# Strassen's scheme for the second product of the last four blocks, with a transposed output stored in short runs

## The chip, the cores and the metric

The kernel runs on one core of one Trainium2 chip. A core has a matrix engine (TensorE, PE), a vector engine (VectorE, DVE), a scalar engine with the transcendental functions (ScalarE, ACT), a general engine (GpSimd, POOL) and an engine that here only issues transfers (SyncE, SP). They run side by side and wait for each other through semaphores. Each engine carries out its own instructions strictly in order. Transfers between DRAM and the on-chip SBUF are issued from a queue of SP, ACT or POOL and carried by 16 DMA engines. PE writes its sums into PSUM, eight banks of 128 x 512 floats. The metric is the device time of one execution, in microseconds (us).

## The reference

Two parts follow each other. The first is a linear attention over 8 batches, 8 heads, 576 positions and 64 features; the second is an RMS norm with a gated feed-forward layer over all 8 x 576 = 4608 tokens of 512 features (d_model), with 1536 hidden features (d_ff).

```python
q_s = softmax(q, over the features)             # exp(q - max) / (sum + 1e-9)
k_s = softmax(k, over the positions)
kv  = einsum('bhsd,bhse->bhde', k_s, v)         # 64 x 64 for each batch and head
x   = einsum('bhsd,bhde->bhse', q_s, kv)        # rearranged to 4608 x 512
xn  = x / sqrt(mean(x * x) + 1e-6) * rms_g
g   = xn @ w_gate                               # 512 x 1536
h   = g * 1 / (1 + exp(-g)) * (xn @ w_val)
out = h @ w_out                                 # 1536 x 512
```

All matrices are wanted in fp32 accuracy. The kernel writes each fp32 operand as a sum of two fp32r numbers, "hi" (a cast) and "lo" (the remainder, a subtraction), and makes a product from three: hi x hi, hi x lo and lo x hi.

## The kernel before

**Blocks and pairs.** The 4608 tokens are worked off in nine blocks of 512. Blocks 0 to 2 go one by one. Blocks 3 to 8 go as three pairs (p = 0, 1, 2; `NPAIR = 3`), and what follows is about them. Names such as `pp` or `put` are steps, each a Python function that issues a few instructions.

**First product of a pair, by Strassen's scheme.** xn of both blocks and the weights are cut in two by two parts. `pp` makes, for each of six groups i of hidden features (two tiles of 128 of each half) and each m (gate or value), seven products of six matmuls instead of eight (L1093). The sums of weights that this needs were made once while blocks 1 and 2 ran, and lie in DRAM ("wd"); `w_in` loads them on POOL's queue. The sums of the activations are `t_add` (L1037), cast and remainder are `b_hi` and `b_lo` (L1049). The results in PSUM are combined on DVE (`c_u2`, `c_u3`, `c_21` and the like, L1114, L1130), `gate` takes the silu on ACT and `hm` multiplies gate by value (L1150). So the hidden tile c (of 12) of block t stands in SBUF with the hidden features on the partitions and 512 tokens along them, 128x512; for t = 0 in tiles "gs", for t = 1 in tiles "xh", "xl" and "w".

**Second product of a pair, plain.** For each block t and hidden tile c, `hp_hi` casts the tile to "hh", `hp_lo` (L1162) makes the remainder "hl", `o_in` loads the tile's 128 x 512 output weights, hi and lo, 512 KB, on POOL's queue, and `f2p` (L1180) makes 12 matmuls: four output tiles of 128 tokens by three terms. After 12 hidden tiles the four sums stand in PSUM with tokens on the partitions. `put` copies each to a tile "ot" (or "gs" at the end, L385, L1193) and stores it with one transfer of 2 KB rows (L1199; for the very last one, two halves on SP's and ACT's queues, L1194 and L1196).

**What sets the order.** All steps stand in one long list, `ORDER`, under a manual schedule: each step is issued where the list has it, on the engine that its letter names (A, D or P for ACT, DVE or POOL). Nothing reorders them later. Tiles of a name come from a pool with a number of buffers ("ot" has 2, "hh" and "hl" 2, "gs" 3); a step that takes a tile whose buffer is still read waits for the reader. The second product of a pair is laced into the first product of the next: in the list, `f2p` steps of pair p stand between the `pp` steps of pair p + 1, and what is left stands alone.

Of the kernel before, what the change touches and what calls it, by code (L numbers as in the profile page):

```python
# [34 lines left out]
k_eps.0.2 q_load0.1.1 k_rec.0.2 q_x0.0.0 kv_norm0.0.3:D kv_norm0.0.2:A k_max.1.0 q_mul0.0.2:P conv_mul.0.2 q_t0.0.3
q_x0.0.1 x_sq.0.0 conv_shift.0.2 x_hi.0.0:A q_t0.0.2 q_c0.0.3:A warm.2.7 conv_mul.1.0 k_tr.1.0 load_w.1.2 q_x0.0.3
q_max0.1.0 x_hi.0.1:A load_w.3.1 q_c0.0.2:D warm.2.4 conv_low.0.2.1 q_sub0.1.0:P load_w.2.1 k_top.1.0 x_sq.0.1 q_x0.0.2
conv_shift.1.0 w_lo.0.1:P q_exp.1.0 x_lo.0.1 n_sum0.0 x_sq.0.3 load_w.2.2 x_lo.0.0 k_diag.1.0:A w_lo.0.0:P n_sum0.1
x_sq.0.2 q_sum0.1.0 x_hi.0.3:A k_rows.1.0 v_load.1.0 n_sum0.2 q_eps0.1.0 conv_low.1.0.2 conv_add.0.2.1 q_max0.1.1
n_sum0.3 q_rec0.1.0 k_sub.1.0 x_hi.0.2:A q_sub0.1.1:P warm.2.12 x_lo.0.3 k_exp.1.0 warm.2.9 n_t.0 conv_mul.2.0  # L40
conv_add.1.0.2 f1.0.0.0.0 f1.0.0.0.1 f1.0.0.0.2 o_hi.0:A n_y0.0 f1.0.0.0.3 f1.0.1.0.0 q_exp.1.1 load_w.4.0 f1.0.0.1.0
x_lo.0.2 f1.0.1.0.1 f1.0.1.0.2 load_w.3.2 f1.0.1.0.3 n_y1.0 f1.0.0.1.1 load_w.3.0 conv_low.2.0.2 f1.0.0.1.2 o_lo.0:P
f1.0.0.1.3 f1.0.1.1.0 f1.0.1.1.1 w_hi.1.0.2:A f1.0.1.1.2 q_load0.1.2 f1.0.1.1.3 q_mul0.1.0:P conv_shift.2.0 f1.0.0.2.0
f1.0.0.2.1 conv_mul.2.1 f1.0.0.2.2 n_rows.0 f1.0.0.2.3 f1.0.1.2.0 w_lo.1.0:P conv_mul.1.2 f1.0.1.2.1 conv_shift.2.1
f1.0.1.2.2 conv_low.1.2.1 f1.0.1.2.3 g_mul.0 conv_mul.4.1 conv_add.2.0.2 q_sum0.1.1 f1.1.0 silu.0 load_w.5.1
conv_shift.4.1 k_load.1.1 conv_shift.1.2 conv_mul.4.0 q_eps0.1.1 h_mul.0 conv_add.1.2.1 w_hi.2.0.2:A load_w.6.0
# [276 lines left out]
def linear_attention_then_gated_ffn(ctx: ExitStack, tc, q, k, v, w_gate, w_val, w_out, rms_g, out):  # L323
# [918 lines left out]
```

## Time and profile before

| | before |
|---|---|
| runs, us | 959.84, 960.16, 964.75 |
| median, us | 960.16 |
| profiled execution, us | 959.09 |
| span in it (first to last instruction), us | 957.2 |
| granted TensorE clock, mean | 0.996 |
| PE busy, us (matmuls) | 936.5 (4697) |
| DVE / ACT / POOL busy, us | 664.1 / 438.3 / 531.7 |

The stretches of the program by their busy time, in us (the program's phases overlap by some microseconds at their ends):

| stretch | PE | DVE | ACT | POOL |
|---|---|---|---|---|
| 0 to 528, blocks 0 to 2 with the attention | 511.3 | 443.6 | 343.7 | 392.7 |
| 528 to 600 | 72.0 | 59.4 | 32.7 | 34.9 |
| 600 to 744 | 144.0 | 70.9 | 26.7 | 49.6 |
| 744 to 888 | 144.0 | 65.3 | 23.5 | 40.4 |
| 888 to 957 | 65.2 | 25.0 | 11.7 | 14.1 |

A profile counts an engine as busy while an instruction of it runs. The "chain" that the text speaks of follows the last instruction of the program back in time, at each step to what released it. "SPq", "ACTq" and "POOLq" are the engines as issuers of transfers. In rows of instructions, `ot<-ps_o 128x512` means that a tile named ot was written from one named ps_o; the bracket behind some rows is the idle time ahead and the work that ended it.

### The profile page before, as it was taken

The page shows a single profiled execution, that of the slowest core. Times are in us where ns is not written, and L with a number is a line of the kernel's source. Part 1 is how long each engine was busy: PE and PEld are TensorE (multiplying, and loading weights), DVE is VectorE, ACT ScalarE, POOL GpSimd, SP SyncE. Part 2 cuts the span into 40 slices and gives each one's busy share as a digit, 9 for nine tenths or more (in the row PEclk, how much of TensorE's full clock was granted, in tenths as well). Part 3 has the DMA queues.
Part 4 walks back from the last instruction along what each step waited for, and adds up shares of the span by engine and source line. Part 5 has one row for each costly group of instructions (what it writes and reads, how often), then busy time and mean ns, then how long its engine had stood idle before and what let it go on. Part 6 is the DMA issues. An engine that isn't in the chain of part 4 may idle for free.

```text
span 957.2 us, 14051 instructions
## 1 busy us (share of the span) xinstructions
PE 936.5 (98%) x4697; PEld 761.8 (80%) x4697; DVE 664.1 (69%) x1424; ACT 438.3 (46%) x703; POOL 531.7 (56%) x551
## 2 busy tenths in 40 slices
PE   7999998999999999999999999999999999999998
PEld 5688886878878887887888888888888888888886
DVE  7899788988879987878887788643436644344442
ACT  5998746766657775565434454101113212111111
POOL 5897856865878887776655436333234311322123
PEclk9999999999999999999999999999999999999999
DMA  9986516889875899887795783756755857546455
GB/s 263 291 255 200 128 36 212 281 283 302 279 247 136 245 262 237 200 255 210 186 259 164 228 247 105 245 160 219 230 198 185 255 168 239 184 151 237 143 155 174
DMA packets 164435, 202.31 MB, mean 211 GB/s; under 512 B 105060, under 2 KB 126860, under 8 KB 159756
## 3 DMA queue, kind: packets, MB, share of 16 engines
q0 software_dynamic: 23232, 113.26, 37.6%
q1 hardware_dynamic: 140988, 88.04, 33.1%
q8 instruction: 37, 0.61, 0.3%
q14 instruction: 34, 0.28, 0.1%
q10 hardware_dynamic: 144, 0.13, 0.0%
HBM read 160.49 MB, written 40.89 MB: 210 GB/s over the span
## 4 chain that ended last, share of the span: by engine, by line
PE 79%; DVE 7%; DMA 7%; SPq 3%; ACT 2%; issue 1%; POOL 0%; DVEq 0%; ACTq 0%; POOLq 0%
PE ps_gv L1093 16%; PE ps_o L1093 12%; PE ps_gv L952 12%; PE ps_o L1180 10%; PE ps_o L989 7%; PE ps_a L1093 6%; PE ps_gv L1180 5%; PE ps_a L1180 5%; SPq L626 3%; DMA kt<-in_k_dram 2%; DMA qt<-in_q_dram 2%; PE ps_a L558 2%; DMA vt<-in_v_dram 1%; PE ps_a L764 1%; DMA w<-in_moe_w_val_dram 1%
## 5 line engine op out<-in xcount | busy, mean ns | idle before, releaser
L952 PE MATMUL ps_gv<-xh,w 128*128 128x512 f32 x576 | 190.2, 398 | 1.2 <-ACT ps_a L434 0.5
L1093 PE MATMUL ps_gv<-x,ring 128*128 128x512 f32 x576 | 142.6, 392 | 0.0
L952 PEld LDWEIGHTS ps_gv<-xh,w 128*128 128x128 f32 x576 | 108.1, 188 | 26.4 <-issue 1.1
L1093 PEld LDWEIGHTS ps_gv<-x,ring 128*128 128x128 f32 x576 | 107.2, 188 | 22.2
L952 PE MATMUL ps_gv<-xl,w 128*128 128x512 f32 x288 | 111.7, 391 | 0.0
L1066 POOL DMA_DIRECT2D ring<-wd x54 | 30.4, 564 | 128.7 <-PE ps_gv L1093 56.8
L1114 DVE TENSOR_TENSOR tmp<-tmp,ps_gv 128x512 f32<-128x512 f32 x84 | 57.2, 682 | 52.1 <-PE ps_gv L1093 49.7
L1093 PE MATMUL ps_o<-x,ring 128*128 128x512 f32 x360 | 84.9, 389 | 0.0
L1093 PEld LDWEIGHTS ps_o<-x,ring 128*128 128x128 f32 x360 | 67.6, 188 | 14.0
L989 PE MATMUL ps_o<-o,hh 128*128 128x512 f32 x288 | 74.9, 403 | 0.0
L385 ACT CAST hh<-gs 128x512 fp32r<-128x512 f32 x56 | 34.5, 616 | 78.1 <-DVE gs L1130 29.4
L952 PEld LDWEIGHTS ps_gv<-xl,w 128*128 128x128 f32 x288 | 54.2, 188 | 10.6 <-issue 0.4
L989 PEld LDWEIGHTS ps_o<-o,hh 128*128 128x128 f32 x288 | 53.3, 190 | 11.2 <-issue 0.4
L1114 DVE TENSOR_TENSOR tmp<-tmp,ps_o 128x512 f32<-128x512 f32 x42 | 28.7, 686 | 42.2 <-PE ps_o L1093 40.0
L876 POOL TENSOR_TENSOR w<-w,w 128x512 fp32r<-128x512 f32 x32 | 43.9, 1375 | 3.9 <-ACT w L385 3.5
L511 DVE TENSOR_REDUCE cm<-kt 116x128 f32<-116x640 f32 x28 | 36.8, 1313 | 4.2 <-DMA kt<-in_k_dram 4.1
L989 PE MATMUL ps_o<-o,hl 128*128 128x512 f32 x144 | 39.4, 396 | 0.3 <-POOL hl L973 0.3
L1162 POOL TENSOR_TENSOR hl<-gs,hh 128x512 fp32r<-128x512 f32 x22 | 28.5, 1298 | 17.0 <-DVE hh L385 9.8
L1180 PE MATMUL ps_o<-o,hh 128*128 128x512 f32 x144 | 37.3, 391 | 0.0
L1093 PE MATMUL ps_a<-x,ring 128*128 128x512 f32 x144 | 37.2, 393 | 0.0
L1066 POOL DMA_DIRECT2D w<-wd x18 | 10.1, 561 | 48.5 <-PE ps_a L1093 23.3
L1093 PE MATMUL ps_a<-x,w 128*128 128x512 f32 x144 | 37.0, 392 | 0.0
(319 smaller groups left out, 2254.7 us busy)
## 6 DMA issues: line engine op xcount, KB each, us to landing
ring<-wd POOLq DMA_DIRECT2D x36, 768.0 KB, 5.0
w<-wd POOLq DMA_DIRECT2D x24, 1024.0 KB, 5.8
o<-od POOLq DMA_DIRECT2D x42, 512.0 KB, 5.2
ring<-wd POOLq DMA_DIRECT2D x18, 1024.0 KB, 5.6
wd<-w SPq DMA_DIRECT2D x12, 1024.0 KB
wd<-parts SPq DMA_DIRECT2D x24, 512.0 KB
ring<-od POOLq DMA_DIRECT2D x18, 512.0 KB, 5.3
x<-od POOLq DMA_DIRECT2D x18, 512.0 KB, 4.9
```

The source lines that it names most:

```text
L385: (e.copy if e is nc.scalar else e.tensor_copy)(dst, src)
L511: nc.vector.tensor_reduce(out=cm, in_=kt_[b, g].rearrange("p h j d -> p h d j"), axis=AX.X, op=ALU.max)
L558: nc.tensor.matmul(pk[h * D:(h + 1) * D, :D + 1], lhsT=ke[:n, h, j], rhs=vt[:n, j, h], start=(j == 0), stop=(j == len(rows) - 1))
L626: nc.sync.dma_start(qt[p0:p0 + 32, c0 // 32:c1 // 32], q[b, 2 * g + h, s0:s0 + c1 - c0, 32 * f:32 * f + 32].rearrange("(m c) i -> c m i", ...
L876: on(nc.gpsimd).tensor_tensor(out=w[:, :, 1], in0=halves(s % NF, a, 1)[:, 0], in1=w[:, :, 0].bitcast(F32), op=ALU.subtract)
L952: nc.tensor.matmul(pd[s], lhsT=w[:, a, c // 2, m, c % 2 * P:c % 2 * P + P], rhs=X[j, c][x], start=(n == 1), stop=(n == 3 * NKT))
L989: nc.tensor.matmul(po[t], lhsT=a[:, t * P:(t + 1) * P], rhs=w, start=(i == 0 and n == 0), stop=(i == NF - 1 and n == len(terms) - 1))
L1066: nc.gpsimd.dma_start(t, src.rearrange("p a b f -> p (a b f)"))
L1093: nc.tensor.matmul(abc[p, i, m, b], lhsT=src[:, h, c * P:(c + 1) * P], rhs=operand(o, c, x), start=first and n == 0, stop=n == 5, skip_gro ...
L1114: nc.vector.tensor_tensor(out=dst, in0=ux[u + (src,)], in1=abc[u + (b,)], op=ALU.add)
L1162: on(nc.gpsimd).tensor_tensor(out=hl, in0=h_src(p, t, c), in1=HH[p, t, c][0].bitcast(F32), op=ALU.subtract)
L1180: nc.tensor.matmul(pa[p, t, k], lhsT=a[:, k * P:(k + 1) * P], rhs=w, start=(c == 0 and n == 0), stop=(c == NF - 1 and n == 2))
```

## The change

The second product of pairs 1 and 2 (blocks 5 to 8) is made by Strassen's scheme too; pair 0 keeps the plain form. Its parts:

- **The product.** `qq` makes one of seven products for one of six groups i: three terms by two halves x of the 256 output features in a quarter, 6 matmuls (L1338). That is 7 x 6 x 6 = 252 matmuls of 128x512 for a pair. The weights are now the stationary operand and the hidden tiles the moving one, so a result has output features on the partitions and 512 tokens along them: turned round against `put`.
- **The activations.** Besides the 24 hidden tiles, four sums for each i are made (`q_t1` to `q_t4`, the last with two operations). Each of the 42 operands is cast (`qb_hi`) and gets its remainder (`qb_lo`, L1323), into five pairs of buffers that are taken in turn. The 24 hidden tiles all live until then, so those of t = 0 get buffers of their own that the attention used ("qt", "qT", "qh", "ql", "acc", "sq", "kt").
- **The weights.** `r_keep` copies w_out to DRAM ("rd"), and in the time of the last attention block and pair 0 `r_load`, `t_sum` (four short additions), `t_hi`, `t_lo` and `t_keep` make four sums for each i, split, in DRAM ("sd"). `qw` loads the weights of one `qq`, 256 KB, on SP's queue, into 11 slots for pair 1 and 19 for pair 2.
- **The results.** Seven products end in five PSUM groups for each half x. `qs1` copies one, `qu2`, `qu3`, `q22`, `q21` and `q12` add others; four results for each x are left (11, 12, 21, 22: quarter of features by block). `qtr` turns each round in 32 x 32 squares on DVE into a buffer "ot" (L1367), and `qput` stores it with four transfers on SP's queue, each 32 partitions by 16 runs of 32 floats, 128 bytes (L1375).
- **`put`** loses its special case for the end, since only pair 0 uses it.
- **`ORDER`** is new from the first step to the last, blocks 0 to 2 included, and the steps' engines with it.

In all the program has 4249 matmul instructions as written, in place of 4321. Transfers issued by SP go from 589 to 763, those by POOL from 156 to 108; tables that ACT loads for its functions from 52 to 62.

The diff's core, with the list and everything that only makes room left out:

```diff
+    STRASSEN2 = 1
...
+        if p >= STRASSEN2 and c not in H1:
+            name, bufs = (("qt", 3), ("qt", 3), ("qt", 3), ("qT", 2), ("qT", 2), ("qh", 2), ("qh", 2), ("ql", 2),
+                          ("ql", 2), ("acc", 1), ("sq", 1), ("kt", 2))[c]
+            H1[c] = ap.tile([P, TB], F32, name=name, bufs=bufs)
+        g_[p, c] = H1[c] if p >= STRASSEN2 else fp.tile([P, TB], F32, name="gs", bufs=3)
...
     def put(p, t, n):
-        last = p == NPAIR - 1 and t == 1
...
+        ot = fp.tile([P, DM], F32, name="ot", bufs=2)
+        copy(ot, pa[p, t, n], nc.vector if n % 2 else nc.scalar)
+        nc.sync.dma_start(ov[blk(p, t), n], ot)
...
+    def qw(p, k, i):
...
+        if k in SUM:
+            nc.sync.dma_start(t.bitcast(F32), sd[i][:, SUM[k]])
+        else:
+            f, h = PLAIN[k]
+            nc.sync.dma_start(t.bitcast(F32), od[2 * i + f][:, :, h * Q:(h + 1) * Q])
...
+    def qb_hi(p, k, i):
...
+        t = HH[p, k, i, 0] = QS[n % 5]
+        copy(t[0], q_src(p, k, i), nc.scalar)
...
+    def qb_lo(p, k, i):
+        t = HH[p, k, i, 0]
+        on(nc.gpsimd).tensor_tensor(out=t[1], in0=q_src(p, k, i), in1=t[0].bitcast(F32), op=ALU.subtract)
...
+    def qq(p, k, i, *xs):
...
+        for n, (l, m) in enumerate(((0, 0), (1, 0), (0, 1))):
+            for x in xs or range(2):
+                nc.tensor.matmul(qacc[p, b, x], lhsT=ws[l][x], rhs=h[m], start=first and i == 0 and n == 0,
+                                 stop=i == NH - 1 and n == 2, skip_group_check=not first)
...
+    def q_comb(p, x, n, dst, src, b):
+        ux[p, "q", x, n] = dst
+        nc.vector.tensor_tensor(out=dst, in0=ux[p, "q", x, src], in1=qacc[p, b, x], op=ALU.add)
...
+    def qtr(p, n, x):
+        src = qacc[p, 0, x] if n == 11 else ux[p, "q", x, n]
+        t = ux[p, "o", x, n] = fp.tile([P, DM], F32, name="ot", bufs=2)
+        nc.vector.transpose(t, src)
+
+    def qput(p, n, x):
+        r, t = n // 10 - 1, n % 10 - 1
+        src = ux[p, "o", x, n]
+        dst = out[blk(p, t) * TB:(blk(p, t) + 1) * TB].rearrange("(j r) d -> r j d", r=32)
+        for g in range(4):
+            c = Q * r + P * x + 32 * g
+            nc.sync.dma_start(dst[:, :, c:c + 32], src[32 * g:32 * g + 32].rearrange("p (j c) -> p j c", c=32))
```

How the order moves, at the places that matter. First the end of DVE's program, before:

```order
L1150 TENSOR_TENSOR w_5873<-w_5873,tmp_4500 128x512
L385 CAST hh_8984<-w_5873 128x512 [waits DVE_49,PE_49]
L385 COPY ot_8986<-ps_o_8045 128x512 [waits DMAHW4_49,DMAHW6_49,DMAHW2_49,DMAHW0_49]
L385 COPY gs_9009<-ps_gv_8798 128x512 [waits PE_49]
L1193 COPY gs_9013<-ps_a_8799 128x256 [waits PE_49]
```

and now (ps_o and ps_a are PSUM results; DMAHW is a transfer that must have landed):

```order
L1367 STREAM_TRANSPOSE ot_9176<-ps_o_8265 128x512 [waits DMAHW5_49,DMAHW4_49,DMAHW6_49,DMAHW3_49,PE_49]
L1347 TENSOR_TENSOR tmp_4512<-tmp_4512,ps_o_8346 128x512
L1367 STREAM_TRANSPOSE ot_9183<-tmp_4512 128x512 [waits DMAHW2_49,DMAHW1_49,DMAHW7_49,DMAHW0_49,DVE_49]
L1367 STREAM_TRANSPOSE ot_9189<-ps_o_8264 128x512 [waits DMAHW5_49,DMAHW6_49,DMAHW4_49,DMAHW3_49]
L1347 TENSOR_TENSOR gs_8955<-gs_8955,ps_a_8877 128x512
L1367 STREAM_TRANSPOSE ot_9196<-gs_8955 128x512 [waits DMAHW2_49,DMAHW1_49,DMAHW7_49,DMAHW0_49,DVE_49]
L1367 STREAM_TRANSPOSE ot_9198<-tmp_4512 128x512 [waits DMAHW5_49,DMAHW6_49,DMAHW4_49,DMAHW3_49]
L1347 TENSOR_TENSOR gs_8953<-gs_8953,ps_a_8876 128x512
L1367 STREAM_TRANSPOSE ot_9205<-gs_8953 128x512 [waits DMAHW2_49,DMAHW1_49,DMAHW7_49,DMAHW0_49,DVE_49]
```

Two copies behind the last matmuls have become six transposes and three additions behind one wait for PE (the results are, in this order, 11, 21 and 11, 12, 21, 12); each transpose also waits for the stores that last read its "ot" buffer. On SP the stores of these six pieces are the program's last 24 transfers; the first two pieces, the third and the last:

```order
L1375 DMA out_0_dram<-ot_9176 32x16x32 [waits DMAHW3_49,DVE_49]
L1375 DMA out_0_dram<-ot_9176 32x16x32 [waits DMAHW4_49]
L1375 DMA out_0_dram<-ot_9176 32x16x32 [waits DMAHW5_49]
L1375 DMA out_0_dram<-ot_9176 32x16x32 [waits DMAHW6_49]
L1375 DMA out_0_dram<-ot_9183 32x16x32 [waits DMAHW7_49,DVE_49]
L1375 DMA out_0_dram<-ot_9183 32x16x32 [waits DMAHW0_49]
L1375 DMA out_0_dram<-ot_9183 32x16x32 [waits DMAHW1_49]
L1375 DMA out_0_dram<-ot_9183 32x16x32 [waits DMAHW2_49]
L1375 DMA out_0_dram<-ot_9189 32x16x32 [waits DMAHW3_49,DVE_49]
...
L1375 DMA out_0_dram<-ot_9205 32x16x32 [waits DMAHW3_49,DVE_49]
...
L1375 DMA out_0_dram<-ot_9196 32x16x32 [waits DMAHW7_49]
```

Before, SP ended with whole tiles, one transfer each; now each tile is four. The third place is DVE between the first product of the second pair and that of the third. Before, where the rest of the second product stands alone:

```order
L1162 TENSOR_TENSOR hl<-gs,hh 128x512 [waits Activation_49]
L1037 TENSOR_TENSOR xh<-xl,xh 128x512
L385 CAST hh<-xh 128x512 [waits PE_49,Pool_49]
L1049 TENSOR_TENSOR x_3660<-xl,x_3660 128x512
L385 CAST hh<-xh 128x512 [waits DVE_49,PE_49]
L1049 TENSOR_TENSOR x_4309<-xl,x_4309 128x512 [waits Activation_49]
L385 CAST x_3820<-xh 128x512 [waits DVE_49]
L1162 TENSOR_TENSOR hl<-xh,hh 128x512 [waits DVE_49,PE_49]
```

and a part of it now (here "qt", "ql" and "qh" hold hidden tiles or their sums, "hl", "vt" and "kv" remainders):

```order
L1323 TENSOR_TENSOR vt<-ql,kt 128x512 [waits PE_49,Activation_49]
L1323 TENSOR_TENSOR hl<-qh,hh 128x512 [waits Pool_49]
L1302 TENSOR_TENSOR qt<-qt,qT 128x512
L1303 TENSOR_TENSOR qt<-qt,xh 128x512 [waits DVE_49]
L1347 TENSOR_TENSOR tmp<-tmp,ps_gv 128x512 [waits PE_49] x2
L1347 TENSOR_TENSOR tmp<-tmp,ps_o 128x512 [waits DVE_49]
L1347 TENSOR_TENSOR tmp<-tmp,ps_o 128x512
L1367 STREAM_TRANSPOSE ot<-tmp 128x512 [waits DMAHW1_49,DVE_49]
L1367 STREAM_TRANSPOSE ot<-tmp 128x512 [waits DMAHW5_49,DMAHW4_49]
L1302 TENSOR_TENSOR ql<-ql,acc 128x512
L1303 TENSOR_TENSOR ql<-ql,w 128x512 [waits DVE_49]
```

The remainders of hidden tiles are joined there by sums of hidden tiles, by the additions of results and by transposes, on the same engine.

More of the change, by code (lines that the diff above doesn't have):

```diff
@@ L1026, in tmp, with tmp_pair @@
         return TMP[name][n % 2]
+    def tmp_pair(name, key, x):
+        if key not in first_turn:
+            tmp(name)
+            first_turn[key] = turn[name]
+            turn[name] += 1
+        return TMP[name][(first_turn[key] + x) % 2]
+    first_turn = {}
     T1 = {}
@@ L1198, in put @@
-        copy(ot, pa[p, t, n], nc.vector if n % 2 else nc.scalar)
-        nc.sync.dma_start(dst, ot)
+        ot = fp.tile([P, DM], F32, name="ot", bufs=2)
+        copy(ot, pa[p, t, n], nc.vector if n % 2 else nc.scalar)
+        nc.sync.dma_start(ov[blk(p, t), n], ot)
+    Q = HALF
+    rd = [tc.dram_tile([P, 2, DM], F32, name=f"rd{i}") for i in range(NH)]
+    sd = [tc.dram_tile([P, 4, 2, Q], F32, name=f"sd{i}") for i in range(NH)]
+    SUM = {6: 0, 7: 1, 3: 2, 5: 3}
+    PLAIN = {1: (0, 0), 2: (1, 0), 4: (1, 1)}
@@ new lines, in linear_attention_then_gated_ffn, with r_keep, r_load, t_sum @@
+    rs2, QS, QW, QV = {}, [], {}, []
+    def r_keep(i):
+        nc.sync.dma_start(rd[i], WW[i].rearrange("p (f a b) -> p f a b", f=2, a=3)[:, :, 2])
+    def r_load(i):
+        rs2[i] = [ap.tile([P, 2, Q], F32, name=n) for n in ("kt", "vt")] + [None, None]
+        for f in range(2):
+            nc.sync.dma_start(rs2[i][f].rearrange("p h m -> p (h m)"), rd[i][:, f])
+    def t_sum(i):
+        a, b = rs2[i][:2]
+        a11, a21, a12, a22 = a[:, 0], a[:, 1], b[:, 0], b[:, 1]
+        e = on(nc.vector)
+        e.tensor_tensor(out=a22, in0=a21, in1=a22, op=ALU.add)
+        e.tensor_tensor(out=a21, in0=a11, in1=a21, op=ALU.subtract)
+        e.tensor_tensor(out=a11, in0=a22, in1=a11, op=ALU.subtract)
+        e.tensor_tensor(out=a12, in0=a12, in1=a11, op=ALU.subtract)
@@ new lines, in q_t1, with q_t2, q_t3, q_t4 @@
+    def q_t1(p, i):
+        a, b = H1[2 * i], h2(2 * i)
+        on(nc.vector).tensor_tensor(out=a, in0=b, in1=a, op=ALU.subtract)
+    def q_t2(p, i):
+        t = ux[p, i, "t2"] = fp.tile([P, TB], F32, name="gs", bufs=3)
+        on(nc.vector).tensor_tensor(out=t, in0=h2(2 * i + 1), in1=H1[2 * i], op=ALU.subtract)
+    def q_t3(p, i):
+        a = h2(2 * i)
+        on(nc.vector).tensor_tensor(out=a, in0=h2(2 * i + 1), in1=a, op=ALU.subtract)
+    def q_t4(p, i):
+        a = H1[2 * i]
+        on(nc.vector).tensor_tensor(out=a, in0=a, in1=H1[2 * i + 1], op=ALU.add)
+        on(nc.vector).tensor_tensor(out=a, in0=a, in1=h2(2 * i + 1), op=ALU.subtract)
@@ new lines, in qb_lo @@
+    def qb_lo(p, k, i):
+        t = HH[p, k, i, 0]
+        on(nc.gpsimd).tensor_tensor(out=t[1], in0=q_src(p, k, i), in1=t[0].bitcast(F32), op=ALU.subtract)
+    qacc = {}
+    QB = {1: 0, 2: 0, 6: 1, 7: 1, 4: 1, 5: 2, 3: 2}
+    def qq(p, k, i, *xs):
+        b = QB[k]
+        first = k in (1, 6, 5)
+        if first and i == 0:
+            for x in range(2):
+                qacc[p, b, x] = ps((BANKS[p % 2][1][3 * x], BANKS[p % 2][1][1 + x], BANKS[p % 2][0][0])[b])
+        w, h = QW[p, k, i], HH[p, k, i, 0]
+        ws = [[w[:, l, x * P:(x + 1) * P] for x in range(2)] for l in range(2)]
+        for n, (l, m) in enumerate(((0, 0), (1, 0), (0, 1))):
+            for x in xs or range(2):
+                nc.tensor.matmul(qacc[p, b, x], lhsT=ws[l][x], rhs=h[m], start=first and i == 0 and n == 0,
+                                 stop=i == NH - 1 and n == 2, skip_group_check=not first)
```

687 lines of the change are left out of this document (375 added, 312 removed).

## The prediction

> **What bounds the kernel now.** I read the page first (busy shares, chain), then the table by stretches of 24 us, then the chain in order of time, and last the timeline of the final microseconds.
>
> ```profile
> span 957.2 us, 14051 instructions
> PE 936.5 (98%) x4697; PEld 761.8 (80%) x4697; DVE 664.1 (69%) x1424; ACT 438.3 (46%) x703; POOL 531.7 (56%) x551
> ...
> PE 79%; DVE 7%; DMA 7%; SPq 3%; ACT 2%; issue 1%; POOL 0%; DVEq 0%; ACTq 0%; POOLq 0%
> ```
>
> TensorE (PE) is busy for 98% of the span, and the chain that ends last is 79% PE.
>
> ```profile
> core 0: us, PE busy (x) PEld busy (x) DVE busy (x) ACT busy (x) POOL busy (x), PEclk, DMA share, GB/s
> 144.00:168.00 24.00, 20.19 (x118) 15.59 (x116) 21.36 (x53) 16.75 (x26) 16.37 (x17) 0.93 0.61 211
> ...
> 192.00:216.00 24.00, 22.82 (x138) 18.35 (x137) 19.60 (x40) 16.27 (x28) 16.74 (x14) 1.00 0.85 280
> ...
> 264.00:288.00 24.00, 22.80 (x117) 17.46 (x116) 18.78 (x38) 14.82 (x25) 18.33 (x16) 1.00 0.77 239
> ...
> 576.00:600.00 24.00, 24.00 (x108) 19.82 (x107) 20.39 (x47) 10.16 (x15) 15.13 (x14) 1.00 0.37 120
> ...
> 744.00:768.00 24.00, 24.00 (x107) 19.89 (x106) 15.35 (x27) 4.72 (x9) 9.35 (x12) 1.00 0.78 238
> ...
> 840.00:864.00 24.00, 24.00 (x108) 19.87 (x107) 10.88 (x15) 4.50 (x8) 7.95 (x11) 1.00 0.48 151
> ```
>
> The columns are the stretch, its length, and each engine's busy time. In the late rows PE has no gap, and VectorE (DVE) has much free time (10.88 of 24 at 840). In the first half PE idles a little: 3.81, 1.18 and 1.20 us in the three stretches shown. So a matmul taken from the last four blocks shortens the span by its own time, unless something takes PE's place.
>
> **Removed: 72 matmuls.** The second product of a pair of blocks now takes 7 x 6 x 6 = 252 matmuls instead of 2 x 12 x 12 = 288, so 36 fewer in each of two pairs. The chain prices them, in the piece where PE did nothing but this product:
>
> ```profile
> 740.98 27.20 PE ps_o L1180 x120
> ```
>
> 27.20 / 120 = 0.2267 us each, and 72 of them make **-16.3 us**. They were all on the bounding engine, so I count them whole.
>
> **Added at the end: a chain of stores.** Before, the last matmul starts at 952.81 and ends at 953.20; 4.0 us later the run is done, with the last store issued at 954.09 to 954.46, that is 2.74 us before the end:
>
> ```profile
> 952.55 0.69 DVE L385 COPY gs<-ps_gv 128x512 f32<-128x512 f32 x1 [4.64 <-PE ps_gv L1180]
> ...
> 952.81 0.39 PE L1180 MATMUL ps_a<-o,hl 128*128 128x512 f32 x1
> 953.23 0.42 DVE L1193 COPY gs<-ps_a 128x256 f32<-128x256 f32 x1
> 953.27 0.33 SPq L1199 DMA_DIRECT2D out_dram<-gs  x1
> ...
> 954.09 0.37 ACTq L1196 DMA_DIRECT2D out_dram<-gs  x1
> ```
>
> Now six transposes and three additions on DVE stand behind the last matmul: the first transpose (C11, half 1) needs it and DVE runs in order, though five of the others wait for nothing that PE still does. They share two "ot" buffers, and each result leaves by four short-run stores on SP's queue. The waits in the order make one chain: the store of 11.1 must land before transpose 11.0 runs; its store before 21.0; that one's before 12.0; then 12.0 and 12.1 are stored. (21.1 and 12.1 fit into the waits.) The new waits are DVE's; nothing but the end stands behind them. The rows for each piece:
>
> ```profile
> L743 DVE STREAM_TRANSPOSE qT<-qt 128x512 f32<-128x512 f32 x28 | 19.5, 699 | 1.5 <-POOL qt L738 1.3
> ...
> 230.91 0.46 SPq L626
> 231.37 0.04 issue
> 231.41 0.46 SPq L626
> 231.87 0.04 issue
> 231.92 1.90 DMA qt<-in_q_dram
> ...
> 258.54 2.66 DMA qt<-in_q_dram
> ...
> 611.16 0.36 SPq L1199 DMA_DIRECT2D out_dram<-ot  x1
> 613.27 0.59 ACT L385 COPY ot<-ps_gv 128x512 f32<-128x512 f32 x1 [11.51 <-DMA out_dram<-ot]
> ```
>
> The loads of q (L626) move the same pieces the other way: 32 partitions, 16 runs of 128 bytes. One takes SP 0.46 + 0.04 = 0.50 us to issue, and the last lands 1.90 to 2.66 us after. A store of long runs landed 613.27 - 611.52 = 1.75 us after its issue. I take 2.2, the middle. A link is then 0.70 (transpose) + 0.03 (hand-over, as from 952.55 + 0.69 to SP's 953.27 above) + 4 x 0.50 + 2.2 + 0.1 (waking) = 5.0; three links 15.1; the end 0.70 + 0.03 + 8 x 0.50 + 2.74 = 7.5; 22.6 in all, against 4.0 before: **+18.6 us**. At the low ends (issue 0.36 + 0.04, landing 1.75) a link is 4.2, the end 6.7, and the growth 15.3. Even with no wait on a buffer, 24 issues of 0.50 would leave 0.05 + 0.73 + 12.0 + 2.74 - 4.0 = +11.5.
>
> **Moved: the vector work.** A pair had 24 casts and 24 remainders for this product and 8 copies out; it now has 42 casts, 42 remainders, 30 sums and at its end 2 copies, 10 additions and 8 transposes. Beside the first product this fits: in the last pair's stage DVE goes from 94 operations to 119, some 64 to 80 us at the prices below, beside 96 x 6 x 0.2267 = 131 us of PE. But thirty of the 42 products stand in one burst behind it. In the burst between the second and the third pair PE has 30 x 6 x 0.2267 = 40.8 us. DVE has 45 operations with two SBUF inputs and 9 with one from PSUM, 4 transposes and 2 casts: 54 x 0.69 + 4 x 0.70 + 2 x 0.47 = 41.0. POOL has 8 at 1.29 = 10.3, ACT 36 x 0.62 = 22.3.
>
> ```profile
> L1162 DVE TENSOR_TENSOR hl<-gs,hh x14: 683/689/1834, 548.2 to 916.6; 128x512 fp32r<-128x512 f32 x14
> L1162 POOL TENSOR_TENSOR hl<-gs,hh x22: 1281/1288/1484, 402.3 to 885.4; 128x512 fp32r<-128x512 f32 x22
> L385 ACT CAST hh<-gs 128x512 fp32r<-128x512 f32 x14 | 8.7, 619 | 50.9 <-DVE gs L1130 26.4 <-PE ps_a L1093 11.1 <-DVE gs L1150 7.1
> L385 DVE CAST hh<-xl 128x512 fp32r<-128x512 f32 x6 | 2.8, 472 | 6.4 <-PE ps_a L1180 4.8 <-PE ps_o L1180 1.6
> ```
>
> DVE is level with PE there, where it had 15.35 of 24 before. The last pair's burst is easier: up to its last matmul DVE has about 38.5 beside 44.9 of PE. What decides is whether POOL's 10.3 us come on top:
>
> ```profile
> 736.48 1.30 POOL L1037 TENSOR_TENSOR xl<-xl 128x512 f32<-128x512 f32 x1
> 736.50 1.83 DVE L1162 TENSOR_TENSOR hl<-gs,hh 128x512 fp32r<-128x512 f32 x1 [0.26 <-ACT hh L385]
> ```
>
> The DVE operation that began beside one of POOL took 1.83 us instead of 0.69: it ended 0.55 us after POOL's. So PE's loss is between 0 and 41.0 + 10.3 - 40.8 = 10.5 us. Half of POOL's operations stand beside DVE's PSUM reads, and a piece of work needed at PE's pace has a few operations of lead, so I take **+3 us**, nearer to the row without a gap. [...]
>
> **At nothing.** The 84 weight loads go from POOL's queue to SP's, 256 KB each, 11 or 19 slots ahead of their product: 15 us of PE, against a landing of some 2 us. Their waits for a free slot also hold the second pair's stores back, which stand between them on SP; DVE's next transpose into the same buffer stands ten or more microseconds of PE behind, so nobody waits. If one did, DVE's additions behind it, and then PE, would stop for a link, 5 us. The sums of the output weights (24 short additions, 12 casts, 12 remainders: about 22 us, most on DVE, between some 540 and 640 us) lie where the row at 576 has the fullest DVE of that part, 20.39 of 24; four such stretches leave 14 us or more, ACT and POOL the rest. If that cover fails, they cost about the difference, 5 us. The new order of blocks 0 to 2 has the same PE work; bounds -6.2 (the three gaps vanish) to +4, value 0.
>
> **Sum.** -16.3 + 18.6 + 3 = +5.3. The profiled execution took 959.09 us (span 957.2); the median shown is 960.16, 1.07 above. So 964.4 beside the profiled time, and **965.5 us** as a median.
>
> **Rivals.**
> *Short landing (not slower).* If stores land and issue at the low ends and the bursts hold, the sum is -16.3 + 15.3 = -1.0: 959.2. For it: the store row of 1.75; against it: long runs there. With the bursts free and issues at 0.50, the change breaks even at a landing of 2.2 - 2.3 / 4 = 1.6 us.
> *The new order mends the first half (not slower).* 3.81 + 1.18 + 1.20 = 6.2 us of gaps vanish: 959.3, faster only with the short landing too, 953.0. For it: gaps exist; against it: the vector engines are as full there as before.
> [...]
> [...]
>
> **How the numbers follow.** Chances: forecast 0.38 (own range 961 to 971), short landing 0.17, first half mended 0.18, port 0.14, double stores 0.13. About 0.5%, 4.8 us, is what a measurement here tells from no change, so the bounds are 955.4 and 965.0. Slower: 0.22 of the forecast, port and double stores, 0.49. Same: 0.16 + 0.12 + 0.07 = 0.35. Faster: 0.05 + 0.11 = 0.16, where both mild cases meet. The range 954 to 977 holds them but for the far ends.
>
> **What would show it.** In the profile after: pieces of 1.36 us a product on PE and 16 us less PE time in all; from the last matmul to the end 22 to 23 us, with four landings of about 2 us in the chain; PE gaps of about 3 us in the burst between the pairs, none in the last; the first half's gaps within some 4 us of today's sum. A tail under 15 us, PE gaps over 8 us in a burst, or a first half shorter by more than 6 us would make the prediction wrong.

## The result and the profile after

The changed kernel takes 974.75 us (median of 4 runs, 974.11 to 976.07), the kernel before 961.35 us (4 runs, 959.84 to 964.75): 1.36% longer, ratio 1.0136 with a 95% interval of 1.0104 to 1.0168. Measured again beside the first experiments it was 974.97 against 960.88, ratio 1.0146 (1.0116 to 1.0176). Three executions in all of these runs ran in a far slower state (1166, 1540 and 3311 us; two of them of the kernel before) and take no part in the ratios.

> The changed kernel once more, as the anchor for the others beside it: 974 to 976 us, the kernel before 960 to 962.

The head of the profile page of the changed kernel, as it was shown of the kernel before:

```profile
span 974.3 us, 14436 instructions
PE 928.1 (95%) x4625; PEld 749.0 (77%) x4625; DVE 739.3 (76%) x1552; ACT 483.8 (50%) x768; POOL 531.1 (55%) x523
...
PE 70%; DMA 12%; DVE 6%; SPq 3%; ACT 3%; issue 3%; POOL 2%; DVEq 0%; ACTq 0%; POOLq 0%
```

PE is busy for 8.4 us less (928.1 against 936.5), but the span is 17.1 us longer, and the chain that ends last has 9 points less of PE and 5 more of transfers. So time went into places where PE waits. To find them I cut both executions at three points that both programs have: the first matmul of pair 0's first product, that of pair 1's, and the end of the last matmul. The first, of the kernel before, and the second, of the changed one, are tables by stretch (stretch, length, busy time of PE and the others, clock, DMA share, GB/s):

```profile
0.00:379.30 379.30, 363.71 (x1985) 289.91 (x1986) 324.06 (x740) 268.22 (x424) 293.11 (x276) 0.99 0.80 230
379.30:587.30 208.00, 206.87 (x1102) 169.38 (x1102) 168.11 (x413) 104.25 (x167) 128.14 (x137) 1.00 0.75 210
587.30:953.20 365.90, 365.89 (x1614) 302.49 (x1612) 171.48 (x272) 65.46 (x113) 110.49 (x138) 1.00 0.60 193
```

```profile
0.00:391.70 391.70, 368.04 (x1984) 290.86 (x1985) 320.55 (x740) 277.74 (x433) 292.55 (x277) 0.99 0.79 230
391.70:597.50 205.80, 204.69 (x1089) 166.99 (x1088) 171.39 (x416) 114.62 (x181) 116.85 (x127) 1.00 0.84 233
597.50:953.60 356.10, 355.33 (x1554) 291.15 (x1552) 241.38 (x389) 91.42 (x155) 121.72 (x120) 1.00 0.66 203
```

| stretch | before, us | after, us | difference | as predicted |
|---|---|---|---|---|
| blocks 0 to 2, up to pair 0 | 379.3 | 391.7 | +12.4 | 0 (-6.2 to +4) |
| pair 0, up to pair 1 | 208.0 | 205.8 | -2.2 | -2.7 (12 matmuls moved out) |
| pairs 1 and 2, to the end of the last matmul | 365.9 | 356.1 | -9.8 | -13.6 (60 matmuls) + 3 |
| last matmul to the end | 4.0 | 20.7 | +16.7 | +18.6 |
| sum | 957.2 | 974.3 | +17.1 | +5.3 |

Three of the four rows are near what the sum had. The first is not: in blocks 0 to 2, where PE has the same matmuls in a new order, PE works 4.3 us longer (368.04 against 363.71; what makes it longer isn't worked out here) and stands 8.1 us longer (23.7 against 15.6).

**The tail.** The chain of waits of the changed kernel at its end (start, length, what):

```profile
953.63 0.73 DVE ot L1367
954.38 0.32 SPq L1375
...
955.82 1.97 DMA out_dram<-ot
957.82 0.05 DVEq L1367
...
957.91 0.73 DVE ot L1367
...
960.21 1.96 DMA out_dram<-ot
...
962.29 0.72 DVE ot L1367
...
964.47 2.00 DMA out_dram<-ot
...
966.69 0.71 DVE ot L1367
```

Here are the three landings, and they stand where the order had them. A link lasts 957.91 - 953.63 = 4.28, then 4.38 and 4.40 us; from the last transpose to the end it is 974.3 - 966.69 = 7.6.

**The burst.** Two rows of the same view at the ends of the burst between pairs 1 and 2, and the busiest stretch of DVE in it:

```profile
735.00 1.37 PE ps_gv L1338 x6
...
776.56 1.39 PE ps_a L1129 x6
```

```profile
744.00:768.00 24.00, 24.00 (x105) 19.43 (x104) 22.93 (x35) 12.09 (x21) 6.65 (x5) 1.00 0.70 188
```

The 180 matmuls between the two rows take 41.56 us, 0.2309 us each in place of 0.2267, and PE has no gap although DVE is busy for 22.93 of 24 us.

**The start.** SP's own issues in the changed kernel, and then the chain of waits there:

```profile
6.74 0.43 SPq L437 DMA_DIRECT2D g_sb<-in_moe_rms_g_dram  x1
14.05 1.41 SPq L522 DMA_DIRECT2D w<-in_v_dram  x2
```

```profile
4.64 5.86 DMA qt<-in_q_dram
...
10.53 0.90 POOL qt L678
...
12.66 1.03 POOL qt L678
13.69 0.28 POOL kv L600 x2
13.97 0.11 POOL w L533 x2
14.08 0.72 SPq L522
```

SP issues nothing from 7.17 to 14.05 us. Its next load, of v, goes into a tile whose last column POOL first fills with ones (L533); in the new order that fill stands on POOL behind two subtractions of q (L678), and the first of those waits for q to land. What SP asks for next, the weights too, is late with it: by 5 to 6 us against the run below that takes this wait away (loads at 15.51, 18.47 and 30.07 us there start at 10.06, 12.84 and 24.81).

### The profile page after: what moved, and what is told of

Same layout as the page of the kernel before. It is cut to its first block, busy times and chain, and to the rows that moved or that the text cites. A ratio compares the mean times of both kernels' runs of the same rounds, so it can differ in the third digit from the quotient of the medians.

```text
span 974.3 us, 14436 instructions
## 1 busy us (share of the span) xinstructions
PE 928.1 (95%) x4625; PEld 749.0 (77%) x4625; DVE 739.3 (76%) x1552; ACT 483.8 (50%) x768; POOL 531.1 (55%) x523
## 4 chain that ended last, share of the span: by engine, by line
PE 70%; DMA 12%; DVE 6%; SPq 3%; ACT 3%; issue 3%; POOL 2%; DVEq 0%; ACTq 0%; POOLq 0%
PE ps_gv L1129 15%; PE ps_o L1129 11%; PE ps_gv L980 10%; PE ps_a L1129 6%; PE ps_o L1338 6%; PE ps_o L1017 5%; PE ps_a L1338 3%; PE ps_o L1222 3%; PE ps_gv L1338 2%; DMA qt<-in_q_dram 2%; PE ps_a L1222 2%; PE ps_gv L1222 2%; DMA kt<-in_k_dram 2%; PE ps_a L584 1%; DMA wd<-w 1%
## 5 line engine op out<-in xcount | busy, mean ns | idle before, releaser
L980 PE MATMUL ps_gv<-xh,w 128*128 128x512 f32 x576 | 192.6, 401 | 5.2 <-DVE w L904 2.5
L1017 PE MATMUL ps_o<-o,hh 128*128 128x512 f32 x288 | 74.1, 399 | 3.5 <-ACT hh L411 2.6
L1017 PEld LDWEIGHTS ps_o<-o,hh 128*128 128x128 f32 x288 | 53.5, 191 | 15.6 <-ACT hh L411 3.5
L904 POOL TENSOR_TENSOR w<-w,w 128x512 fp32r<-128x512 f32 x38 | 51.7, 1368 | 14.2 <-ACT w L411 14.1
L1001 POOL TENSOR_TENSOR hl<-gs,hh 128x512 fp32r<-128x512 f32 x25 | 34.8, 1394 | 19.4 <-ACT hh L411 18.1
L411 ACT CAST hh<-gs 128x512 fp32r<-128x512 f32 x47 | 28.8, 615 | 13.3 <-DVE gs L1172 5.2
L1129 PE MATMUL ps_gv<-x,w 128*128 128x512 f32 x144 | 35.3, 392 | 0.0
L411 ACT COPY tmp<-ps_a 128x512 f32<-128x512 f32 x18 | 10.5, 584 | 48.1 <-PE ps_a L1129 44.7
```

The lines of the kernel that those rows point to most:

```text
L411: (e.copy if e is nc.scalar else e.tensor_copy)(dst, src)
L904: on(nc.gpsimd).tensor_tensor(out=w[:, :, 1], in0=halves(s % NF, a, 1)[:, 0], in1=w[:, :, 0].bitcast(F32), op=ALU.subtract)
L980: nc.tensor.matmul(pd[s], lhsT=w[:, a, c // 2, m, c % 2 * P:c % 2 * P + P], rhs=X[j, c][x], start=(n == 1), stop=(n == 3 * NKT))
L1001: on(nc.gpsimd).tensor_tensor(out=hl, in0=g_[s], in1=h_[s][0].bitcast(F32), op=ALU.subtract)
L1017: nc.tensor.matmul(po[t], lhsT=a[:, t * P:(t + 1) * P], rhs=w, start=(i == 0 and n == 0), stop=(i == NF - 1 and n == len(terms) - 1))
L1129: nc.tensor.matmul(abc[p, i, m, b], lhsT=src[:, h, c * P:(c + 1) * P], rhs=operand(o, c, x), start=first and n == 0, stop=n == 5, skip_gro ...
```

## The experiments

### The start: one fill, one load

The first experiment moves three steps on POOL and nothing else:

```diff
-... k_max0.0.0 q_sub0.0.0:P ... q_sub0.0.1:P ... kv_zero.4 v_ones.0.2 v_load.0.2 ... v_ones.0.0 v_load.0.0 ... v_ones.0.1 v_load.0.1
+... k_max0.0.0 v_ones.0.2 v_ones.0.0 v_ones.0.1 q_sub0.0.0:P ... q_sub0.0.1:P ... kv_zero.4 v_load.0.2 ... v_load.0.0 ... v_load.0.1
```

> The changed kernel with three fills of ones (for value tiles 2, 0 and 1) put ahead of the first two subtractions of q on POOL, nothing else. Theory A1 (the start is late because the first load of v waits on SP for a fill that stands on POOL behind subtractions that wait for q; SP issues nothing from 7.17 to 14.05 us): the loads of v start near 8 us, the first matmul of the gated layer starts 4 us earlier, near 34.4 us, and 4 to 5 us come back at the end, 970 us. Rival A2 (the loss of 5 us between 72 and 96 us is also a late result of that stall): 10 us come back, 965 us. Rival A3 (the stall is hidden, DMA is the limit at the start anyway): 974 us.

Measured: 970.92 us, ratio 1.0102 (1.0078 to 1.0125); 4.05 us less than the changed kernel's 974.97. SP's row for the first load of v, now right behind the one before it:

```profile
7.05 0.43 SPq L397 DMA_DIRECT2D g_sb<-in_moe_rms_g_dram  x1
7.64 1.64 SPq L482 DMA_DIRECT2D w<-in_v_dram  x2
```

Theory A1 holds: the place of these fills on POOL was worth 4 us at the end of the program. How far a kernel is behind the kernel before, I read from the start of the n-th matmul of the gated layers in the profiled execution; all these kernels have the same 1272 of them ahead of pair 0. The orders differ, so a point in the midst can be off by 2 or 3 us; in the last row all have done the same work.

| n-th matmul, its time before | changed, second run | fills first | both moves (below) | both moves, early tail (the last run) |
|---|---|---|---|---|
| 130, 67.4 us | 5.3 | -0.1 | -0.3 | 3.2 |
| 210, 87.9 us | 10.0 | 6.4 | 2.8 | 6.1 |
| 370, 128.9 us | 10.9 | 7.4 | 3.7 | 7.0 |
| 800, 250.0 us | 12.6 | 9.1 | 5.2 | 8.1 |
| 1273, pair 0's first, 379.3 us | 13.1 | 10.4 | 5.8 | 9.0 |

With the fills first the lag of the first 67 us is gone, but by 88 us it is 6 us again. PE in that stretch of this run, in order of time, and the stretch by busy time:

```profile
76.11 2.07 PE L940 MATMUL ps_gv<-xh,w 128*128 128x512 f32 x4 [3.20 <-DVE w L864]
77.98 3.62 PE L977 MATMUL ps_o<-o,hh 128*128 128x512 f32 x8
81.40 1.32 PE L977 MATMUL ps_o<-o,hl 128*128 128x512 f32 x4
```

```profile
72.00:84.00 12.00, 8.80 (x46) 6.56 (x45) 7.16 (x15) 8.59 (x13) 8.11 (x7) 0.72 0.70 245
```

PE waits 3.20 us, and then the next four matmuls take 77.98 - 76.11 = 1.87 us and the eight behind them 81.40 - 77.98 = 3.42 us, 0.43 to 0.47 each in place of 0.23; the granted clock of the stretch is 0.72. So a gap of 3.2 us cost some 6 (an estimate: 3.20 + 1.87 + 3.42 - 12 x 0.23 = 5.7). What was late is one load of output weights, which ACT needs in its order:

```profile
72.32 0.62 ACT L420 ACTIVATE ps_a<-raw 128x512 f32<-128x512 f32 x1 [4.34 <-DMA raw<-in_moe_w_out_dram]
```

In the new order it stands on SP behind the first short-run load of q (eight transfers, 9.1 us) and behind a load whose buffer ACT must first give free. The next run moves that one step:

```diff
-... q_load.2.0 ... load_w.8.0 ... load_w.5.2
+... load_w.5.2 q_load.2.0 ... load_w.8.0
```

> The changed kernel with the three fills ahead of the first subtractions of q, as before, and one load more moved: the output weights of tile 5 are asked for ahead of the first short-run load of q instead of behind it and a load that waits for ACT. In the run with the fills alone this load was issued at 66.9 us and landed at 72.3, ACT waited 4.3 us for it and PE 3.2 us at 76 us, and then the next twelve matmuls took 4.5 us in place of 2.7. Theory J (the second loss of the start is that load): the lag behind the kernel before stays under 2 us up to 130 us, 8 to 9 us come back of the changed kernel's time, 966 us (ratio 1.005). Rival K (something else of the new order is late there): the lag at 130 us is still 5 us or more, 971 us (ratio 1.010).

Measured: 967.7 us, ratio 1.0074 (1.0042 to 1.0106), between the two forecasts and nearer to theory J; the profiled execution is 3.7 us behind at 129 us, where the two said under 2 and 5 or more, so J's sign came only in part. PE's gap at that place is 0.88 us in place of 3.20. So the two moves, of the fills and of a load, account for about 7 of the 12.4 us: 974.97 - 967.7 = 7.3 by the medians, 13.1 - 5.8 = 7.3 by the last row of the table, and 963.43 - 955.74 = 7.7 between the two runs below that have the early tail. The 4 us of the fills are clear of the noise, since the four executions with them (969.5 to 971.5) lie below all of the changed kernel's beside them (972.6 to 977.4). The load's 3 us are less sure: the six executions with both moves run from 966.2 to 973.4.

One profile alone says little here. The last run has the same steps at its start as this one, and its profiled execution, the slowest of its four, is 3 us later from the first row of the table on.

### The start: the old order put in

These runs take the old order up to some step, put the six copies of the output weights (`r_keep`) where the new order has them, and go on with the new order.

> The changed kernel with the old order of the steps up to the ninth-last second product of block 2 (some 375 us); what the change adds there, the six copies of the output weights to DRAM and the merged tile of the key-value matrices, stays. Theory A (the new order of blocks 0 to 2 costs the time: the first product of pair 0 begins at 391.7 us instead of 379.3): 12.4 us come back, 962 us, and that product begins near 380 us. Rival B (what the change adds to this stretch costs it: the merged tile ties steps together, the copies take the queue): 972 us or more, the product still begins past 388 us.

Measured: 979.81 us, ratio 1.0197 (1.017 to 1.0223), which neither theory said. (The cut stood ahead of the third-last second product of block 2, not the ninth-last.) Up to the splice the run was 4 to 7 us behind (4.3 at 129 us, 6.6 at 305), not 11 to 14; at the splice PE stood for 11 us, because the two lists ask for loads of q and k in another order:

```profile
PE ps_a L512 <- DVE cm L497: 11.1, 1, 11.1
```

So this run tells nothing of the time, and the next was cut where both lists have issued the same loads.

> The changed kernel with the old order of the steps up to the twelfth second product of block 0 (some 160 us), cut where both orders have asked for the same loads, so that no load is late where the two lists meet; all that the change adds stays. Theory A (the new order of the start loses 10 us by 96 us, and the rest of blocks 0 to 2 nothing more): 10 us come back, 965 us, and pair 0's first product begins near 382 us. A weaker form (the old order loses 3 to 4 us there too, as up to the splice in the run before): 968 us. Rival B (what the change adds to blocks 0 to 2 costs the time, not the order of the start): 972 us or more.

Measured: 968.69 us, ratio 1.0078 (1.0047 to 1.011), the weaker form. Up to 146 us the run is at most 1.2 us behind the kernel before, although it has the merged tile; of the six copies only one lies ahead of the splice. Behind the splice it loses some 3 us, is 7.9 us behind at 250 us, and pair 0's first product begins at 385.9 us, not near 382. With a later cut:

> As the run with both at once, but with the old order kept up to the fifth second product of block 2 (some 310 us) in place of 160 us, and the early tail on two queues. The first half was late by 0.5 us up to 150 us with the old start and by 3.5 to 6 us from 240 us on. Theory F (those 3 to 6 us are the new order as well): pair 0 begins within 2 us of the kernel before, and the time is 3 us below the run with both, 955 us. Rival G (they come from what the change adds there, the copies of the output weights and the merged tile, or from the splice): the lag is 4 us or more again by 300 us, 958 us or more.

Measured: 961.79 us, ratio 1.0007 (0.9985 to 1.0029). Its profiled execution (966.60 us) was 3.8 us behind at 47 us already, where the other three runs with the same steps there were 0.9, 1.2 and 4.3 behind, and it lost 9 us more at its splice (one wait of 5.3 us for a tile of k). So neither the time nor the start of pair 0 (394.7 us) settles F or G. But up to its splice this run keeps the old order, and it still goes from 3.8 us behind at 129 us to 7.4 at 305. The run with the old order up to 375 us goes from 4.3 to 6.6. In both, 2.2 us of it are lost in the same two places, at 196 and at 220 us of the kernel before. The kernels of the table, all in the new order, lose 2.7 to 3.6 us between the same two points. So this part of the loss comes with the old order too: that speaks against F and for G, or for something else that all these runs share. Which added step costs it stays open.

### The tail

The six late pieces get a buffer each, from tiles that nothing reads any more; the order stays:

```diff
-        t = ux[p, "o", x, n] = fp.tile([P, DM], F32, name="ot", bufs=2)
+        late = p == NPAIR - 1 and n != 22
+        if late:
+            name = {(11, 1): "qt", (21, 1): "qt", (11, 0): "qt", (12, 1): "qT", (21, 0): "qT", (12, 0): "qh"}[n, x]
+            t = ap.tile([P, DM], F32, name=name, bufs=3 if name == "qt" else 2)
+        else:
+            t = fp.tile([P, DM], F32, name="ot", bufs=2)
+        ux[p, "o", x, n] = t
```

> The changed kernel with the six late results of the last pair turned round into six buffers of their own (from tiles that nothing reads any more) instead of two, the order unchanged. Theory C (three landings of about 2.0 us in the chain hold the transposes): no transpose waits for a store, the end is set by 24 issues at 0.52 us on SP, 0.04 + 0.73 + 12.5 + 2.0 = 15.3 us from the last matmul to the end instead of 20.7: 5.4 us less, 969.4 us. Rival D (the short runs load the DMA engines so that stores queue up behind each other): landings grow to 4 us or more and 2 us or less come back, 973 us.

Measured: 972.26 us, ratio 1.0118 (1.0091 to 1.0146), and by the trace 16.4 us from the last matmul's end (953.96) to the end (970.4) in place of 20.7. The six transposes follow one another without a wait, and the 24 issues run from 954.74 to 967.68 without a gap, 0.54 us each. Theory C holds by the trace: the landings were 4.3 us of the tail, and behind them stands the issue. By the time, 2.7 us came back, which is nearer to rival D's 973 than to C's 969.4; but the last landing ends 970.4 - 967.68 = 2.7 us behind its issue, not 4 or more. The stretch in the midst of it:

```profile
960.00:964.00 4.00, 0.00 (x0) 0.00 (x0) 0.00 (x0) 0.00 (x0) 0.00 (x0) 0.50 0.80 120
```

Next, each piece is turned round as soon as its sums stand, 21 and 12 before the last product, 11 at the end, once with all stores on SP and once with half of each piece's four issued by ACT:

```diff
-... q21.2.0 ... qq.2.3.5 ... qq.2.2.5.1 qtr.2.11.1 q21.2.1 qput.2.11.1 qtr.2.21.1 ...
+... q21.2.0 qtr.2.21.0 qput.2.21.0 ... qb_lo.2.3.5:D q21.2.1 qtr.2.21.1 qput.2.21.1 ... qq.2.3.5 q12.2.0 qtr.2.12.0 ...
+            e = nc.scalar if late and g % 2 else nc.sync
```

> The changed kernel with the late results of the last pair in six buffers of their own, turned round as soon as their sums stand (21 and 12 before the last product ends, 11 last), and half of each result's four transfers issued by ACT. Theory C (the tail was the chain of landings and then SP's 24 issues): from the last matmul to the end 0.04 + 0.73 for the last transpose, some 1.2 us until both queues are through, 2.0 to 2.7 us of landing: 4.0 to 5.0 us instead of 20.7, so 959 us. Rival D (the DMA engines are the limit with short runs, 1.5 MB in a few microseconds): 10 us or more of tail, 964 us.

> The changed kernel with the early tail and six buffers, but all stores on SP. In the run with two queues the tail was 9.3 us, not 4 to 5. Theory H (the DMA engines limit it: short runs move some 130 GB/s at a full share, 1.5 MB in 12 us from the first store at 938 us on): one queue ends at most 1.5 us later than two, tail 9 to 11 us, 963 to 965 us. Rival I (the issue limits it: 22 issues of 0.53 us after 944 us are 11.7 us): tail 12 us or more, 966 us.

Measured: two queues 963.43 us, ratio 1.0003 (0.9982 to 1.0025), tail 959.5 - 950.2 = 9.3 us; one queue 964.75 us, ratio 1.0036 (1.0016 to 1.0056), tail 960.6 - 950.7 = 9.9 us. With two queues that is level with the kernel before, with one 0.4% slower; the tail is twice what theory C gave for two queues and near rival D's 10 us. With two queues the DMA engines were nearly full for some microseconds (columns as above; share 0.94, 133 GB/s):

```profile
948.00:952.00 4.00, 2.21 (x10) 1.46 (x8) 3.16 (x5) 0.00 (x0) 0.00 (x0) 1.00 0.94 133
```

So 128-byte runs moved 133 / 0.94 = 141 GB/s at a full share here. In the kernel before, while q was loaded in 128-byte runs too, it was 55 / 0.43 = 128:

```profile
350.00:352.00 2.00, 2.00 (x26) 1.64 (x26) 1.79 (x9) 1.97 (x3) 1.33 (x2) 1.00 0.43 55
```

At 141 GB/s the 1.57 MB of the six pieces take some 11 us (an estimate), whoever issues them. SP stood from 951.2 to 954.8 us with its last four issues. In the list of its program each of its transfers waits for the one eight before it, and whether that or the full engines held it isn't told apart here. With one queue, SP's last eight issues and a stretch beside them:

```profile
953.63 4.29 SPq L1341 DMA_DIRECT2D out_dram<-qt  x8
```

```profile
952.00:956.00 4.00, 0.00 (x0) 0.00 (x0) 0.00 (x0) 0.00 (x0) 0.00 (x0) 0.98 0.82 120
```

SP issues its last 20 transfers from 947.19 to 957.92 us with hardly a gap, 0.54 us each, and the engines' share is 0.82. So theory H has the right number (one queue ends 0.6 us later than two), but with one queue what is busy without a break is the issue, as rival I has it. The two limits lie close together here, and H isn't shown for one queue.

How dear the short runs are, the next run shows. It stores each of the six pieces with one transfer of 128 rows of 2 KB, without turning the tokens back into their places (so the rows of the last two blocks stand elsewhere, and a part of the last block isn't written):

```diff
+        if p == NPAIR - 1 and n != 22:
+            nc.sync.dma_start(ov[blk(p, t), 2 * r + x], src)
+            return
```

> The changed kernel with each of the six late results of the last pair stored by one transfer of 128 rows of 2 KB in place of four of short runs. Left out: the turning back of the blocks of 32 tokens into their places, so the last two blocks of the output stand in another order. What the short runs cost: theory C (a link is transposing, issuing, landing): three links of 0.73 + 0.03 + 0.40 + 1.75 + 0.1 = 3.0 and an end of 0.73 + 0.03 + 0.80 + 2.7 = 4.3, 13.3 us of tail instead of 20.7, 967.6 us. Rival E (most of a link is the landing itself and is the same for both kinds): 972 us.

Measured: 967.03 us, ratio 1.0042 (1.0014 to 1.0069), tail 967.9 - 954.7 = 13.2 us, as theory C had it (13.3). Its chain and a stretch of it:

```profile
954.73 0.73 DVE ot L1327
...
955.48 2.05 DMA out_dram<-ot
...
957.55 0.73 DVE ot L1327
```

```profile
958.00:962.00 4.00, 0.00 (x0) 0.00 (x0) 2.83 (x5) 0.00 (x0) 0.00 (x0) 0.67 0.29 108
```

A link is 2.82 us in place of 4.28. The landing is the same, 2.05 us against 1.97; the difference is that there is one issue in place of four. And 108 GB/s take a share of 0.29, so 372 GB/s at a full one: by these two rows the short runs used the DMA engines 372 / 141 = 2.6 times as long.

### Both together

The old order of the first 160 us with the early tail on two queues, and then the two moves of the start with the same tail, in the new order without a splice:

> Both at once: the old order of the first 160 us and the early tail on two queues. If the two losses are separate and the 72 matmuls are worth what they were counted (16.3 us less some 4 us of slower products and small gaps): 974.9 - 10 - 15.9 = 949 us, 1.2% faster than before; with 3 to 4 us lost at the start all the same: 952.5 us. If the matmuls taken out were not on the path (PE waits elsewhere as soon as the tail is short): 960 us, as before.

> The same two moves with the early tail on two queues, all other steps in the changed kernel's order (no splice). By theory J and the 11.5 us that the tail gave: 955 us, ratio 0.993 to 0.995. By rival K: 960 us, ratio 0.999.

Measured: 958.57 us, ratio 0.9956 (0.9934 to 0.9978), and **955.74 us, ratio 0.9929 (0.9906 to 0.9953)**, 5.4 us faster than the kernel before (961.16 beside it). The last is theory J's number, though its profiled execution (958.64) is still 9.0 us behind at pair 0's first product. The first came out 6 us or more above its forecasts, since the tail stayed at 9.3 us and not 4 to 5 and the order behind the splice lost some 5 us again; but the matmuls that the change takes out were on the path: that run begins pair 0's first product 6.2 us behind the kernel before (385.5 against 379.3) and ends its last matmul 8.4 us ahead of it (944.8 against 953.2). The loss at the start and the loss at the end add up separately: 7.3 us came back with the two moves alone, 11.5 with the early tail alone, 19.2 with both.

## Why the prediction was right or wrong

The time, 974.75 us, lies in the range of 954 to 977 and on the side, slower, that had the greater chance; the likeliest case, 965.5, was 9 us short, and its growth of 5.3 us was really 13.4 by the medians and 17.0 between the profiled executions (976.07 against 959.09). That it lies in the range is luck: the range went up to 977 for a burst that loses the whole 10.5 us (973.0; "port" among the chances) and for short stores at half the rate of the loads of q (976.0; "double stores"), neither of which came, and most of what was missing came from a term put at nothing.

- **Removed, -16.3: right in count, somewhat less in time.** The 72 matmuls are gone, but PE's own work from pair 0 on fell by 12.7 us (572.76 to 560.02), not by 16.3. The matmuls of the new product took 0.2309 us in the burst, not 0.2267; over the 504 of them that is 2.1 us, an estimate. The other 1.5 us I can't place.
- **The tail, +18.6: right in mechanism, 1.9 too much.** Three landings in the chain, as the order showed; 4.3 us a link in place of 5.0. The landing of 1.97 us counts from the start of the fourth issue, whose 0.5 us I had added to it, and the chain's first issues took 0.32, not 0.50.
- **The burst, +3: near, by another cause.** Pairs 1 and 2 gave back 9.8 us of 13.6, a loss of 3.8. PE's gaps in the whole stretch are only 0.8 us (356.10 - 355.33); 2.1 us are the dearer matmuls just named, and about 1 us is part of what I can't place. So the size fits by luck. The loss of 10.5 us that the chances call "port" (0.14) did not come to pass: DVE was busy for 22.93 of 24 us and PE had none of its gaps there. Beside POOL's operations two of DVE's additions of tiles in SBUF took 1.67 and 1.64 us in place of 0.69 (at 756.47 and 762.17 of the changed kernel; what held them isn't shown), while two pairs of additions from PSUM took 1.28 us a pair (at 746.26 and 759.62).
- **At nothing, the new order of blocks 0 to 2: this step failed.** "The new order of blocks 0 to 2 has the same PE work; bounds -6.2 (the three gaps vanish) to +4, value 0" measured +12.4. The same PE work doesn't bound what an order costs: the lower bound was taken from PE's gaps before, which limit only the gain, and the +4 had no row behind it. Seven of the 12.4 us come back with two moves, of fills of ones on POOL and of a load on SP; both could be read in the list: what stands on POOL ahead of the fill for which the first load of v waits, and what stands on SP ahead of a load that ACT needs next. I read the order at the tail and in the burst, and not at the start. Of the rest, 2 to 4 us are lost with the old order too, and what causes them is open.
- **The rivals.** The case of "double stores", which had a chance of 0.13, was wrong: the landing was 1.97 us, and the rate from the loads of q, 128 GB/s, was near the 141 found; the halving was my guess, and no run shows it. That a piece's issue of 2 us hides its transfer (256 KB, 1.9 us at 141 GB/s, an estimate) fits this and isn't tested. Once the stores started early on two queues, that rate filled the DMA engines to 0.94. "Short landing" was right on the landing alone. "The new order mends the first half" had the sign wrong.
- **The signs it named.** The tail (20.7 us for 22 to 23) and the pieces of a product (1.37 us for 1.36) came near. PE's time fell by 8.4 us and not by 16, PE had 0.8 us of gaps and not 3 in the last two pairs, and the first half's gaps grew by 8.1 us, twice the 4 allowed. The last one points at the new order by itself.

## What to carry to other kernels

An order that is new from the first step is an edit at the start too: read each queue's first rows and ask for every wait what now stands ahead of its releaser on that engine, because late loads there moved the whole program here (4.05 us at its end for those behind the fills, some 3 us for that of the output weights). A saving on the bounding engine is only had if the end of the program has no new chain (here PE was busy for 8.4 us less, and the time behind the last matmul grew by 16.7): count landings between the last matmul and the end, and start the stores that don't need the last product before it. Splicing two orders to test one of them costs time of its own where they meet (11 us, 9 us, and some 3 us even where both had asked for the same loads), so moving single steps in one order told more.

## What the runs showed of the hardware

- A gap of 3.20 us on PE was followed by twelve matmuls at 0.43 to 0.47 us in place of 0.23 (the run with the fills first, 76 to 81 us; granted clock 0.72 over the 12 us), and in the tail of the run with six buffers, where PE has nothing to do, the granted clock is 0.50 (the row at 960:964 above).
- Stores in runs of 128 bytes moved 141 GB/s at a full share of the DMA engines (0.94 and 133 GB/s in the row at 948:952), in runs of 2 KB 372 GB/s (0.29 and 108 GB/s in the row at 958:962), which is 2.6 times as much. One transfer landed as fast in both: 1.97 us for 64 KB in short runs and 2.05 us for 256 KB in long ones.
